# Two PSUM banks for the last block's third token group, and a front laid out in another order

## The chip, the cores and the metric

The kernel runs on one core of a Trainium2 chip. The metric is device time in microseconds (us) of one execution. The kernel before takes 789.9 us (median of three runs, 789.57 to 794.27).

## What is computed

Three stages run one behind the other, all in float32. Four batches of 576 positions with 8 heads of 64 go through an attention that works with 32 landmarks, whose small matrix is inverted by six Newton steps. Its 2304 rows of 512 then pass two feed-forward layers of width 2048:

```
q_lm, k_lm = means of 18 positions each          # 32 landmarks
A, Bm, C = sm(q, k_lm), sm(q_lm, k_lm), sm(q_lm, k)
Z = Bm.T / (norm1(Bm) * norminf(Bm))
for _ in range(6): Z = 2 * Z - Z @ Bm @ Z
x = A @ Z @ C @ v                                # as 2304 x 512
h = x @ w_in;   x = (h * clip(h + 3, 0, 6) / 6) @ w_out          # layer 1
h = x @ w2_in                                                    # layer 2
P = a0 + a1*h + a2*h**2 + a3*h**3
Q = 1 + |b0|*|h| + |b1|*h**2
out = (P / (Q + 1e-6)) @ w2_out
```

## The kernel before

Matrix products of the two layers are made of three passes each: an operand is split into a rounded high part and the rest (`hi`, `lo`), and hi x hi, hi x lo and lo x hi are added in PSUM. So each product of a 128x128 weight tile is three matmuls.

**Front.** Everything up to the seventh unit of layer 2 is written as Python generators ("steps"), each cut into pieces by `yield`. The list `ORDER` names, entry by entry, which step advances next; each engine executes its instructions in the order in which they were so written. `SLOTS` says which PSUM bank and which SBUF slab each tile of the front takes. Parts of the front that matter below: `warm` (L361, matmuls on an identity that fill waits), the attention's scores (L352), its transposes (L566, L569), `first_v` (L599, the product with v, two calls for batch 0), the Newton steps (L551 on TensorE, L588, L633 and L637 on VectorE, L631 on ScalarE), layer 1's first product (L717, with L721, L724, L727, L730 behind it) and second product (L747), its results with the first half added (L774), and the conversion of weights from raw bits (L230 on ScalarE, L236 on VectorE) and their split (L246, L249). All DMAs are issued on SP, in the same list's order.

**Layer 2.** Tokens are worked in 6 blocks (`j`) of 384, each in 8 units (`u`) of two 128-wide chunks (`i`) of the hidden dimension. For unit n, `l2_in` makes h (24 matmuls 128x384, L822), `l2_poly`, `l2_exp`, `l2_mul` and `l2_split` make the gate and its two parts, and `l2_out(n - 2)` multiplies with `w2_out`: for each of the two chunks and each of three groups of 128 tokens (`m` = 0, 1, 2), three matmuls into the group's PSUM bank `po0`, `po1`, `po2`. The sums run over all 16 chunks of a block. `po0` has two buffers, used by turns from block to block; `po1` and `po2` have one. Behind a block's last unit the banks are read out times -1 (L904 on VectorE, L906 on ScalarE) and stored (L907 on SP).

In the last block the third group is read out in two column halves, both by VectorE. Only its very last chunk (n = 47, i = 1) is also multiplied in two halves of 256 columns, into the two halves of one bank; the chunks before it are multiplied 512 columns wide.

Of the kernel before, what the change touches and what calls it, by code (L numbers as in the profile page):

```python
# [9 lines left out]
F32 = mybir.dt.float32  # L10
# [7 lines left out]
AF = mybir.ActivationFunctionType  # L18
# [9 lines left out]
DM, DFF = 512, 2048  # L28
NT = B * S
P = 128  # L30
HB = S // 2
NFC = DFF // P
NDC = DM // P
T2 = 384
NB2 = NT // T2
# [13 lines left out]


ORDER = [int(x) for x in """
# [72 lines left out]
""".split()]  # L124

SLOTS = [[int(x) for x in s.split()] for s in ("""
# [13 lines left out]
""")]  # L140

# [6 lines left out]
def fused(ctx: ExitStack, tc: tile.TileContext, qT, kT, v, w_in, w_out, w2_in, w2_out, ca, cb, out):  # L148
    nc = tc.nc
    V, A, G, PE, SP = nc.vector, nc.scalar, nc.gpsimd, nc.tensor, nc.sync  # L150
# [641 lines left out]
    L2P = {}  # L792
# [8 lines left out]
    NN = NB2 * NU2  # L801
# [73 lines left out]
    ops = {}  # L875

    def l2_out(n):
        j, u = divmod(n, NU2)
        if u == 0:
            ops[j] = [L2P["ps"].tile([P, 512], F32, tag=f"po{m}", name="po", bufs=2 if m == 0 else 1) for m in range(3)]  # L880
        t = s2.pop((n, "hl"))
        halves = [slice(0, DM // 2), slice(DM // 2, DM)]
        for i in range(2):
            c = 2 * u + i
            for m in range(3):
                for s in halves if n == NN - 1 and i == 1 and m == 2 else [slice(0, DM)]:
                    for k, (xp, wp) in enumerate(((0, 0), (0, 1), (1, 0))):
                        PE.matmul(  # L888
                            ops[j][m][:, s], t[:, xp, i, m * P:(m + 1) * P],
                            w2o[u][wp][:, i * DM + s.start:i * DM + s.stop],  # L890
                            start=(c == 0 and k == 0), stop=(c == NFC - 1 and k == 2 and s.stop == DM),
                        )
        if u == NU2 - 1:
            ps3 = ops.pop(j)

            for m in (1, 2, 0) if j < NB2 - 1 else (0, 1, 2):
                ps = ps3[m]
                o = L2P["p"].tile([P, DM], F32, tag="o", name="o", bufs=3)
                rows = out[j * T2 + m * P:j * T2 + (m + 1) * P, :]

                cs = halves if j == NB2 - 1 and m == 2 else [slice(0, DM)]
                for h, c in enumerate(cs):
                    if m == 0 or len(cs) == 2:
                        V.tensor_scalar(o[:, c], ps[:, c], -1.0, None, op0=ALU.mult)  # L904
                    else:
                        A.activation(o[:, c], ps[:, c], AF.Copy, scale=-1.0)  # L906
                    SP.dma_start(rows[:, c], o[:, c])  # L907

    def open_units():
# [35 lines left out]
    for x, j in convs:  # L945
        f, w = srcs[x]
# [85 lines left out]
    for n in range(LAID):  # L1032
        for i in cuts(n):
            at(l2_in, n, i)
            at(l2_poly, n, i, V if n == 0 or (n, i.start) == (1, 0) else G)
        for i in cuts(n - 1) if n else ():
            at(l2_split, n - 1, i)
        for i in cuts(n):
            at(l2_exp, n, i)
        for i in cuts(n):  # L1040
            at(l2_mul, n, i)
        if n >= 3:
            at(next_split, 1, n - 3)
        if n >= 2:
            at(l2_out, n - 2)
# [16 lines left out]
    for n in range(LAID, NN + 2):  # L1062
        j, u = divmod(n, NU2)
        if n < NN and u == 0 and j + 1 < NB2:
            L2P["load"](j + 1)
        for i in cuts(n):
            run(l2_in, n, i)
            run(l2_poly, n, i, G)
        for i in cuts(n - 1):
            run(l2_split, n - 1, i)  # L1070
        for i in cuts(n):
            run(l2_exp, n, i)
        for i in cuts(n):
            run(l2_mul, n, i)
        u0 = 3 if j == 0 else 2
        if n < NN and j + 1 < NB2 and u0 <= u < u0 + NDC:
            run(next_split, j + 1, u - u0)
        run(l2_out, n - 2)
# [51 lines left out]
```

## Time and profile before

| | |
|---|---|
| median of three runs | 789.9 us |
| profiled execution, its own time | 789.22 us |
| its span, first to last instruction | 787.4 us |
| TensorE busy in it | 777.1 us (99%) |
| VectorE, ScalarE, GpSimd busy | 561.7, 473.9, 323.2 us |
| granted TensorE clock | 1.0 of full speed throughout |

Matmuls overlap in the trace (a 128x512 one lasts 0.39 us and the next starts 0.23 us behind its start), so that times between starts are used below, not durations. A row that ends in "x2" merges neighbours. SPq rows are DMA issues. The engine names are PE (TensorE), DVE (VectorE), ACT (ScalarE), POOL (GpSimd) and SP.

### The profile page before, as it was taken

Reading aid. Unit: us, or ns where it says so; the run is one execution under the profiler, and the core shown is the slowest. Engines: PE = TensorE matmul, PEld = TensorE weight load, DVE = VectorE, ACT = ScalarE, POOL = GpSimd, SP = SyncE. Lnnn points to the kernel's source line nnn. Section 1 sums busy time; section 2 is a strip of 40 time slices with the busy share of each in tenths; the row PEclk is TensorE's granted clock in tenths of the full one; section 3 lists DMA queues with packets and bytes.
Section 4 is the critical chain, followed back from the end, with each engine's and each line's share of the span. In section 5 each row is a group of like instructions: output and inputs, shape, how many; then the busy total and the mean of one; then the engine's idle time right before and its main releaser. Section 6 shows DMA issues by size and latency. Waiting matters only on the chain.

```text
span 787.4 us, 15172 instructions
## 1 busy us (share of the span) xinstructions
PE 777.1 (99%) x6037; PEld 704.6 (89%) x6037; DVE 561.7 (71%) x975; ACT 473.9 (60%) x892; POOL 323.2 (41%) x230
## 2 busy tenths in 40 slices
PE   8999999999999999999999999999999999999998
PEld 3599989999899999999998889989989989989896
DVE  7888988894655477567889776765766766766665
ACT  3888746554555446567674665566656656656553
POOL 2583400000000000000289768657666765775574
PEclk9999999999999999999999999999999999999999
DMA  9998587647234666556400110110101011000001
GB/s 342 389 357 336 175 331 256 240 146 255 63 95 158 228 209 212 173 179 188 145 2 1 40 41 1 41 41 1 41 1 40 2 41 41 1 0 15 28 1 40
DMA packets 42471, 96.38 MB, mean 122 GB/s; under 512 B 5792, under 2 KB 22432, under 8 KB 42400
## 3 DMA queue, kind: packets, MB, share of 16 engines
q1 hardware_dynamic: 42400, 95.41, 35.2%
q8 instruction: 47, 0.77, 0.4%
q14 instruction: 24, 0.20, 0.1%
HBM read 73.38 MB, written 22.02 MB: 121 GB/s over the span
## 4 chain that ended last, share of the span: by engine, by line
PE 90%; DVE 6%; ACT 1%; DMA 1%; issue 1%; SPq 0%; POOL 0%; DVEq 0%; ACTq 0%
PE psy L747 25%; PE po L888 24%; PE ph L822 24%; PE psh L717 12%; PE psa L352 3%; DVE w2s L285 1%; PE psa L599 1%; DMA qx<-in_q 1%; PE psa L551 1%; DVE val L236 1%; DVE g L864 1%; DVE p L860 0%; DVE q L858 0%; PE psa L566 0%; PE psy L361 0%
## 5 line engine op out<-in xcount | busy, mean ns | idle before, releaser
L873 POOL TENSOR_TENSOR g2hl<-g,g2hl 128x768 fp32r<-128x768 f32 (+1 forms) x53 | 92.2, 1741 | 306.3 <-ACT g2hl L871 306.2
L747 PE MATMUL psy<-ghl,whi 128*128 128x288 f32 x1024 | 209.8, 298 | 0.1
L822 PE MATMUL ph<-yhl,w2h 128*128 128x384 f32 x768 | 195.7, 335 | 0.0
L888 PE MATMUL po<-w2h,g2hl 128*128 128x512 f32 x578 | 188.3, 394 | 1.3 <-POOL g2hl L873 1.2
L747 PEld LDWEIGHTS psy<-ghl,whi 128*128 128x128 f32 x1024 | 162.9, 188 | 7.8 <-issue 5.0
L747 PE MATMUL psy<-ghl,wlo 128*128 128x288 f32 x512 | 150.2, 293 | 0.0
L822 PEld LDWEIGHTS ph<-yhl,w2h 128*128 128x128 f32 x768 | 139.8, 188 | 3.8
L888 PEld LDWEIGHTS po<-w2h,g2hl 128*128 128x128 f32 x578 | 108.5, 188 | 25.4 <-POOL g2hl L873 1.9
L822 PE MATMUL ph<-yhl,w2s 128*128 128x384 f32 x384 | 128.9, 336 | 0.0
L858 DVE SCALAR_TENSOR_TENSOR q<-q,r 128x768 f32<-128x768 f32 (+1 forms) x53 | 51.6, 973 | 107.8 <-ACT r L853 106.8
L717 PE MATMUL psh<-AT,us 128*128 128x288 f32 x768 | 117.7, 296 | 0.0
L888 PE MATMUL po<-w2s,g2hl 128*128 128x512 f32 x289 | 113.4, 392 | 0.0
L717 PEld LDWEIGHTS psh<-AT,us 128*128 128x128 f32 x768 | 107.0, 188 | 0.7 <-DVE g L724 0.4
L836 POOL TENSOR_SCALAR q<-t,cab 128x768 f32<-128x768 f32 (+1 forms) x50 | 65.4, 1308 | 97.9 <-ACT t L832 97.9
L747 PEld LDWEIGHTS psy<-ghl,wlo 128*128 128x128 f32 x512 | 96.2, 188 | 0.0
L838 POOL TENSOR_TENSOR q<-q,t 128x768 f32<-128x768 f32 (+1 forms) x50 | 91.1, 1822 | 4.0
L851 ACT ACTIVATE r<-q,lnb 128x768 f32<-128x768 f32 (+1 forms) x53 | 46.5, 877 | 73.3 <-POOL q L838 72.7
L721 ACT ACTIVATE r<-psh,three 128x288 f32<-128x288 f32 x128 | 61.9, 494 | 43.7 <-PE psh L717 43.0
L727 ACT ACTIVATE ghl<-g 128x288 fp32r<-128x288 f32 x128 | 55.0, 441 | 52.6 <-DVE g L724 41.5
L832 ACT ACTIVATE t<-ph 128x384 f32<-128x384 f32 x96 | 46.9, 489 | 56.3 <-PE ph L822 56.3
L724 DVE SCALAR_TENSOR_TENSOR g<-r,psh 128x288 f32<-128x288 f32 x128 | 56.8, 449 | 31.2 <-ACT r L721 29.8
L822 PEld LDWEIGHTS ph<-yhl,w2s 128*128 128x128 f32 x384 | 72.1, 188 | 0.0
(150 smaller groups left out, 1039.9 us busy)
## 6 DMA issues: line engine op xcount, KB each, us to landing
raw<-in_moe_w_out SPq DMA_DIRECT2D x32, 511.8 KB, 6.9
raw<-in_moe_w_in SPq DMA_DIRECT2D x32, 511.5 KB, 8.0
wis<-wid SPq DMA_DIRECT2D x24, 512.0 KB, 5.1
kx<-in_k SPq DMA_DIRECT2D x8, 576.0 KB, 6.1
yd<-y SPq DMA_DIRECT2D x32, 144.0 KB, 3.4
out<-o SPq DMA_DIRECT2D x17, 256.0 KB, 2.0
vx<-in_v SPq DMA_DIRECT2D x4, 1024.0 KB, 7.9
wid<-val SPq DMA_DIRECT2D x8, 512.0 KB, 5.7
```

The costliest lines, as they stand in the source:

```text
L717: PE.matmul(ps[:, :HB], u[:, wp, f0:f0 + P], at[:, xp, g, :], start=(k == 0), stop=(k == 5))
L721: A.activation(r, ps[:, :HB], AF.Relu, bias=three)
L724: V.scalar_tensor_tensor(gg, in0=r, scalar=6.0, in1=ps[:, :HB], op0=ALU.min, op1=ALU.mult)
L727: A.activation(t[:, 0, :], gg, AF.Copy)
L747: PE.matmul(ps[e][:, :HB], w1[c // 2][wp][:, o + e * P:o + (e + 1) * P], t[:, xp, :], start=(c == c0 and i == 0), stop=(c == c1 and i == 2),)
L822: PE.matmul(ps[i][:, :T2], w2i[u][wp][:, d * 256 + i * P:d * 256 + (i + 1) * P], yh[:, xp, d, :], start=(k == 0), stop=(k == 11),)
L832: A.activation(t[:, i], h, AF.Abs)
L836: eng.tensor_scalar(q[:, cs], t[:, cs], cb_s[:, 1:2], cb_s[:, 0:1], op0=ALU.mult, op1=ALU.add)
L838: eng.tensor_tensor(q[:, cs], q[:, cs], t[:, cs], op=ALU.mult)
L858: V.scalar_tensor_tensor(q, in0=q, scalar=QC, in1=r, op0=ALU.add, op1=ALU.mult)
L873: G.tensor_tensor(t[:, 1, i], g, t[:, 0, i].bitcast(F32), op=ALU.subtract)
L888: PE.matmul(ops[j][m][:, s], t[:, xp, i, m * P:(m + 1) * P], w2o[u][wp][:, i * DM + s.start:i * DM + s.stop], start=(c == 0 and k == 0), s ...
```

## The change

First, in block 5 a fourth bank is taken, from the two buffers of `po0`; it holds columns 256 to 511 of the third group, while `po2` holds columns 0 to 255. All 16 chunks of that group are multiplied in two halves. The first half is read out by VectorE, the second by ScalarE.

```
-            ops[j] = [L2P["ps"].tile(..., bufs=2 if m == 0 else 1) for m in range(3)]
+            ops[j] = [L2P["ps"].tile(..., bufs=2 if m == 0 else 1)
+                      for m in ((0, 1, 2) if j < NB2 - 1 else (0, 1, 2, 0))]
...
-                for s in halves if n == NN - 1 and i == 1 and m == 2 else [slice(0, DM)]:
+                for h, s in enumerate(halves if j == NB2 - 1 and m == 2 else [slice(0, DM)]):
                     for k, (xp, wp) in enumerate(((0, 0), (0, 1), (1, 0))):
                         PE.matmul(
-                            ops[j][m][:, s], t[:, xp, i, m * P:(m + 1) * P],
+                            ops[j][m + h][:, s], t[:, xp, i, m * P:(m + 1) * P],
...
-                            start=(c == 0 and k == 0), stop=(c == NFC - 1 and k == 2 and s.stop == DM),
+                            start=(c == 0 and k == 0), stop=(c == NFC - 1 and k == 2),
...
-                    if m == 0 or len(cs) == 2:
+                    if m == 0 or len(cs) == 2 and h == 0:
                         V.tensor_scalar(o[:, c], ps[:, c], -1.0, None, op0=ALU.mult)
                     else:
-                        A.activation(o[:, c], ps[:, c], AF.Copy, scale=-1.0)
+                        A.activation(o[:, c], ps3[m + h][:, c], AF.Copy, scale=-1.0)
```

Second, the first part of `ORDER`, and `SLOTS` with it, holds other numbers; the rest of the table stays as it was. Two of its lines:

```
-3 5 3 6 0 3 3 8 7 3 9 123 8 12 15 124 124 125 11 16 10 10 11 11 11 10 108 2 24 25 1 11 11 11 11 108 110 25 108 11 11
+3 5 3 6 0 3 3 8 7 3 9 123 8 12 15 124 124 11 125 16 10 10 11 11 11 10 108 2 24 25 1 11 11 11 11 108 110 25 108 11 11
```

Lines behind the change move down by one: L888, L904, L906 and L907 become L889, L905, L907 and L908.

On TensorE the first difference stands in batch 0's Newton steps. Before, both calls of `first_v` (L599, writing `psa` from `vx` and `eT`) stand together, ahead of a Newton step (L551, writing `psy`) and its two fill matmuls (L361); the piece of the difference:

```order
-L599 MATMUL psa<-vx,eT 32x64 x40
-L551 MATMUL psy_431<-ev_87 32x64 x8
-L361 LDWEIGHTS ident
-L361 MATMUL psy_143<-ident 128x512
-L361 LDWEIGHTS ident
-L361 MATMUL psy_143<-ident 128x512
+L599 MATMUL psa<-vx,eT 32x64 x20
+L551 MATMUL psy_410<-ev_87 32x64 x8
+L361 LDWEIGHTS ident
+L361 MATMUL psy_143<-ident 128x512
+L361 LDWEIGHTS ident
+L361 MATMUL psy_143<-ident 128x512
+L599 MATMUL psa<-vx,eT 32x64 x20
```

The second call has moved behind that step and its fill.

On VectorE the rows between batch 1's first Newton matrix (L588, writing `ev_86`) and its second (L637) read, before:

```order
L588 SCALAR_TENSOR_TENSOR ev_86<-psa,rc,id_75 128x32 x2
L724 SCALAR_TENSOR_TENSOR g<-r,psh 128x288
L633 TENSOR_TENSOR ev_87<-ev_86,id_75 128x2x32
L542 TENSOR_SCALAR rc<-csm 128x2
L543 RECIPROCAL rc<-rc 128x2
L544 SCALAR_TENSOR_TENSOR rc<-rc 128x2
L730 TENSOR_TENSOR ghl<-g,ghl 128x288
L577 COPY eT<-psa 64x128
L730 TENSOR_TENSOR ghl<-g,ghl 128x288
L724 SCALAR_TENSOR_TENSOR g<-r,psh 128x288
L637 TENSOR_TENSOR ev_86<-psa,ev_87 128x2x64
```

and now:

```order
L588 SCALAR_TENSOR_TENSOR ev_86<-psa,rc,id_75 128x32 x2
L236 SCALAR_TENSOR_TENSOR val<-raw,top_83 128x512
L724 SCALAR_TENSOR_TENSOR g<-r,psh 128x288
L542 TENSOR_SCALAR rc<-csm 128x2
L543 RECIPROCAL rc<-rc 128x2
L544 SCALAR_TENSOR_TENSOR rc<-rc 128x2
L730 TENSOR_TENSOR ghl<-g,ghl 128x288
L774 SCALAR_TENSOR_TENSOR y<-psy,ypart 128x288
L724 SCALAR_TENSOR_TENSOR g<-r,psh 128x288
L633 TENSOR_TENSOR ev_87<-ev_86,id_75 128x2x32
L637 TENSOR_TENSOR ev_86<-psa,ev_87 128x2x64
```

L633, for which a TensorE Newton step waits, has moved from the second place behind L588 to the ninth. On TensorE, twelve matmuls L747, then eight transposes L566, now stand between the step that reads `ev_86` and the one that reads `ev_87`:

```order
L551 MATMUL psa<-ev_86 32x32 x8
L747 MATMUL psy<-ghl,whi 128x288 x2
L747 MATMUL psy<-ghl,wlo 128x288
L747 MATMUL psy<-ghl,whi 128x288 x2
L747 MATMUL psy<-ghl,wlo 128x288
L747 MATMUL psy<-ghl,whi 128x288 x2
L747 MATMUL psy<-ghl,wlo 128x288
L747 MATMUL psy<-ghl,whi 128x288 x2
L747 MATMUL psy<-ghl,wlo 128x288
L566 MATMUL psa<-ident,e 128x128 x8
L551 MATMUL psa<-ev_87 32x64 x8
```

Before, nine matmuls L747, six L717, four transposes and one L569 stood there. Likewise twelve L747 stand now between the step that makes the first matrix (L551, reading `bm`; L588 reads its result) and the step that reads `ev_86`; before it was six.

## Rows read from the trace of the kernel before

**Rows 1.** Page, part 1: busy time, share of the span and instructions by engine.

```profile
PE 777.1 (99%) x6037; PEld 704.6 (89%) x6037; DVE 561.7 (71%) x975; ACT 473.9 (60%) x892; POOL 323.2 (41%) x230
```

**Rows 2.** Waits of PE, whole span, the longest: total us, times, longest us.

```profile
PE po L888 <- POOL g2hl L873: 1.2, 1, 1.2
```

**Rows 3.** Busy time, us and (instructions), of the reordered part but its first 8 us.

```profile
core 0: us, PE busy (x) PEld busy (x) DVE busy (x) ACT busy (x) POOL busy (x), PEclk, DMA share, GB/s
30.00:115.00 85.00, 84.89 (x991) 76.55 (x986) 73.77 (x146) 64.26 (x138) 38.54 (x34) 1.00 0.84 309
```

**Rows 4.** Timeline of PE, batch 0's first product with v: start us, us, instruction.

```profile
23.64 1.13 PE L599 MATMUL psa<-vx,eT 64*32 64x64 f32 x44 [1.21 <-issue]
```

**Rows 5.** Timeline of PE, batch 1's first Newton steps (the first L551 reads bm).

```profile
95.44 0.33 PE L551 MATMUL psa<-bm 32*32 32x32 f32 x16
95.70 0.53 PE L747 MATMUL psy<-ghl,whi 128*128 128x288 f32 x2
96.07 0.29 PE L747 MATMUL psy<-ghl,wlo 128*128 128x288 f32 x1
96.20 0.42 PE L747 MATMUL psy<-ghl,whi 128*128 128x288 f32 x2
96.46 0.29 PE L747 MATMUL psy<-ghl,wlo 128*128 128x288 f32 x1
96.69 0.33 PE L551 MATMUL psa<-ev 32*32 32x32 f32 x16
96.94 0.66 PE L566 MATMUL psa<-ident,e 128*128 128x128 f32 x4
97.36 0.52 PE L747 MATMUL psy<-ghl,whi 128*128 128x288 f32 x2
```

**Rows 6.** Timeline of DVE, the same place.

```profile
96.01 0.40 DVE L588 SCALAR_TENSOR_TENSOR ev<-psa,rc,id 128x32 f32<-128x32 f32 x2
96.34 0.44 DVE L724 SCALAR_TENSOR_TENSOR g<-r,psh 128x288 f32<-128x288 f32 x1
96.70 0.21 DVE L633 TENSOR_TENSOR ev<-ev,id 128x64 f32<-128x64 f32 x1
96.83 0.16 DVE L542 TENSOR_SCALAR rc<-csm 128x2 f32<-128x2 f32 x1
...
97.30 0.45 DVE L730 TENSOR_TENSOR ghl<-g,ghl 128x288 fp32r<-128x288 f32 x1
```

**Rows 7.** Groups by form, DVE, 30 to 115: count | busy us, mean ns | idle before.

```profile
L236 DVE SCALAR_TENSOR_TENSOR val<-raw,top 128x512 uint32<-128x512 uint32 x28 | 22.1, 804 | 2.7 <-ACT top L230 2.7
```

**Rows 8.** Timeline, first second-layer output of block 5 (PE), block 4's po0 (DVE).

```profile
729.26 0.68 DVE L904 TENSOR_SCALAR o<-po 128x512 f32<-128x512 f32 x1
730.13 0.64 PE L888 MATMUL po<-w2h,g2hl 128*128 128x512 f32 x2
```

**Rows 9.** Timeline of PE, the last 57 matmuls, all on line L888: first and last.

```profile
770.81 0.39 PE L888 MATMUL po<-w2h,g2hl 128*128 128x512 f32 x1
...
782.43 0.51 PE L888 MATMUL po<-w2h,g2hl 128*128 128x512 f32 x2
782.78 0.28 PE L888 MATMUL po<-w2s,g2hl 128*128 128x256 f32 x1
...
783.25 0.28 PE L888 MATMUL po<-w2h,g2hl 128*128 128x256 f32 x1
```

**Rows 10.** Timeline, reads of the last block's second bank and third.

```profile
782.86 0.60 ACT L906 ACTIVATE o<-po 128x512 f32<-128x512 f32 x1 [3.06 <-PE po L888]
...
783.57 0.76 DVE L904 TENSOR_SCALAR o<-po 128x256 f32<-128x256 f32 x2 [0.71 <-PE po L888]
```

**Rows 11.** Timeline of SP, the last three issues: start us, us.

```profile
783.48 0.33 SPq L907 DMA_DIRECT2D out<-o  x1
...
784.02 0.33 SPq L907 DMA_DIRECT2D out<-o  x1
...
784.44 0.40 SPq L907 DMA_DIRECT2D out<-o  x1
```

More of the change, by code (lines that the diff above doesn't have):

```diff
@@ L879, in l2_out @@
         if u == 0:
-            ops[j] = [L2P["ps"].tile([P, 512], F32, tag=f"po{m}", name="po", bufs=2 if m == 0 else 1) for m in range(3)]
+            ops[j] = [L2P["ps"].tile([P, 512], F32, tag=f"po{m}", name="po", bufs=2 if m == 0 else 1)
+                      for m in ((0, 1, 2) if j < NB2 - 1 else (0, 1, 2, 0))]
         t = s2.pop((n, "hl"))
```

56 rows, old and new, of tables (ORDER, SLOTS) are left out of this document.

## The prediction

> **What bounds the kernel now.** I read the page's first part before anything else. TensorE is busy for 777.1 us of a span of 787.4 us, 99% [rows 1]; the next engine, VectorE, for 71%. So only what makes TensorE work longer or shorter, or wait, can move the time, and the two ends of the span where it doesn't work yet or any more. Next the list of TensorE's waits: the longest wait on a semaphore is 1.2 us, for GpSimd at L888 in layer 2 [rows 2], at a place that the change leaves alone. Then the window over the reordered part: from 30 to 115 us TensorE is busy 84.89 of 85.00 us, VectorE 73.77, ScalarE 64.26, and the granted clock is 1.00, full speed, 2.4 GHz [rows 3]. The reader is to see there that a better order has 0.11 us to win in these 85 us, and that VectorE, with 87% of them taken, has little room if work is put ahead of something that TensorE waits for. Last I read single rows: the start of the Newton steps, where TensorE stands idle for 1.21 us with no semaphore behind it ("issue") [rows 4], and the end, where the last matmul starts at 783.25 and lasts 0.28, to 783.53 [rows 9], so that 3.87 us of reads and stores follow it up to 787.4.
>
> The profiled execution took 789.22 us, 1.8 us more than its span; the median of the three runs is 789.9, 0.7 us above it. I work out a difference against the span and put it on the median.
>
> **The change part by part.**
>
> *Split matmuls.* Block 5 has 16 chunks; the last was split already, so 15 chunks change three matmuls of 512 columns into six of 256: 45 more instructions in pairs, the columns stay the same. Start to start, 50 intervals of 512 wide lie between 770.81 and 782.43, 0.2324 us each; from the second 256-wide start, 782.78, to the last one, 783.25, are four, 0.1175 us each [rows 9]. A pair takes 0.2350, so a split costs 0.0026 us, and 45 cost 0.12 us. This is measured on the same operands and place, so I take it. Bounds: nothing below; above, by the nearest other row, a 288-wide matmul takes half of 96.46 - 96.20, 0.13 us [rows 5], and if 256 columns took as much a split would cost 0.028 us and all of them 1.2 us.
>
> The Trainium skill speaks against splitting here: its page "TensorEngine Tiling (Array Packing)", section "Instruction Overhead", gives each matmul an overhead of about 60 cycles. If every one of the 45 added matmuls paid it, an estimate from that page's figure at 2.4 GHz is 25 ns each and 1.1 us in all, where the rows on the six halves at the end give 0.12; the trace doesn't show that overhead in matmuls that follow one another.
>
> *The fourth bank.* It is the `po0` buffer that block 4 used. VectorE reads it out from 729.26 to 729.94 [rows 8]. The second matmul of the row at 730.13 opens the third group of block 5, some 0.23 us behind, at 730.36; its first half comes first, three matmuls of 0.1175, so the new bank is written from about 730.7, 0.8 us after it is free. Cost nothing; without that lead it would be the excess of VectorE's read. Later blocks don't exist, so nothing waits for the extra bank.
>
> *The end.* Before, both halves were read after the very last matmul, since they lay in one bank with one stop: VectorE 783.57 to 784.33, two reads [rows 10]. SP issued the second group's store at 783.48, half 0's at 784.02 and half 1's at 784.44 [rows 11]; the span ends 2.96 us after this last issue. Now half 0 is complete after the third of the six 256-wide matmuls, which ends at 783.53 less three intervals, about 783.18, and VectorE reads it while TensorE still works; it is done by about 783.6. Half 1 is read by ScalarE, free since 782.86 + 0.60 = 783.46, from 783.57; it takes at most the 0.60 us of the 512-wide read [rows 10], to 784.17, and at least the 0.4 that VectorE takes for a half, to 783.97. SP limits what this gives: two issues in a row are 0.42 us apart (784.02, 784.44). So half 0's is issued at 783.90 and half 1's at 784.32, 0.12 us earlier than now. I take -0.12 us. Bounds: if SP's spacing didn't hold, 783.97 + 0.05 against 784.44 would be -0.4; if ScalarE took more than 0.72 us, nothing.
>
> *The front's order.* TensorE executes the same matmuls in it, so its length there changes only by waits and by what neighbours cost each other. The second I can price: where a run of wide matmuls is left for small ones, the start after the last wide one comes 0.23 us behind (96.46 to 96.69) instead of 0.13, and on the way back three matmuls span 0.37 (95.70 to 96.07) instead of 0.26 [rows 5]. One excursion costs 0.2 us. I counted in the two orders how often a product of layer 1 is left for small matmuls and returned to: 36 before, 35 now. That gives -0.2 us; with a doubt of two excursions either way, -0.6 to +0.2.
>
> The split of `first_v` at the start moves a Newton step between its two calls. The 1.21 us of idle stand inside the first call (44 of the row's matmuls follow it) with nothing released at its end [rows 4], so the same matmuls meet the same gap. Cost nothing; if the gap were gone, -1.2.
>
> The risky place is batch 1's first Newton matrix. VectorE's L633, which the second step reads, has moved from behind one L724 to behind seven instructions more. By durations, from L588's start: 0.40 for both L588, 0.80 for L236 [rows 7], 0.44 for L724, 0.47 for the three small ones (96.83 to 97.30), 0.45 for L730, 0.44 for L774 (priced as L724, the same 128x288 read of PSUM), 0.44 for the second L724, 0.21 for L633 [rows 6]: 3.65 us. L588 starts 0.57 us behind the step that feeds it (95.44 to 96.01), so the matrix is there 4.2 us after that step's start. TensorE, from the same start: 0.26 for the step, twelve L747 at 0.13, 0.25 for the step that reads `ev_86`, twelve more L747, and eight transposes at 0.105 (four from 96.94 to 97.36) [rows 5]: 0.26 + 1.56 + 0.25 + 1.56 + 0.84 = 4.5 us. The matrix comes 0.3 us early, so the added wait is nothing. But this holds only if VectorE reaches L588 as promptly as before. Each us by which it is later than 0.3 us is a us of TensorE; behind L633 on VectorE stand L637 of the next step and the copies of the transposes, so the next Newton steps would be late too. I take 0; bounds -0.1 (the 0.11 us of the window) and +2.5 (two of L236 and two of L724 late at once).
>
> **Sum.** +0.12 - 0.12 - 0.2 + 0 = -0.2 us. The span becomes 787.2, the profiled execution about 789.0, the median 789.7.
>
> **The rivals.**
>
> *The new order makes TensorE wait (slower than before).* At the place just described, or at a later Newton step: before, VectorE is 87% busy there [rows 3], and the lead of 0.3 us is less than one L236. For it: seven more instructions ahead of L633. Against it: the order before kept TensorE fed all through with the same load on VectorE. A lag of VectorE of 1 to 3 us there costs 0.7 to 2.7 us; in the middle 1.7, so 791.4 us. It decides from a lag of 0.3 us on. For a loss over 1% it would need 8 us of lag, ten L236 in a row.
>
> *The split costs what narrow matmuls cost elsewhere.* By the bound above 1.2 us for 0.12, so 790.8. For it: matmuls of 288 columns take 0.13. Against it: the halves of the last chunk, the very same instructions, take 0.1175. The overhead in the Trainium skill ("TensorEngine Tiling (Array Packing)", "Instruction Overhead") would make this rival true, at an estimated 790.7.
>
> *The idle at the start goes away.* With a Newton step and its fill in between, what TensorE lacked for 1.21 us would arrive behind other work [rows 4]: 789.7 - 1.2 = 788.5. For it: no semaphore ended that idle, so it can depend on what is fetched or issued just then, and the order after it is another. Against it: nothing ahead of the gap has changed on TensorE.
>
> *The end gives nothing.* If the two stores wait for each other, or ScalarE's read takes over 0.72 us, the 0.12 us are missing: 789.8, which can't be told from the forecast and is counted with it.
>
> **How the numbers follow.** The forecast, all terms as summed: 0.61; own range 789.2 to 790.3, from the bounds of the excursions and the end. A wait in the front: 0.20, 790.4 to 792.4. Costly splits: 0.06, 790.8. The idle gone: 0.13, 788.5. The range 788.2 to 792.0 takes in all but the far end of the waits. About what a measurement of this kernel can tell from no change is 1%, 7.9 us: nothing that I priced gets there. Faster by over 1% would need all of what TensorE doesn't work in the span: 0.02. Slower by over 1% needs a lag of 8 us or several waits on end: 0.04. Within 1%: 0.94.
>
> **What would show it.** Split: the intervals of 256-wide matmuls in block 5, over 45 pairs, stay at 0.1175; at 0.13 the second rival holds. Fourth bank: no wait of TensorE at its first half but one shorter than 0.1 us. End: VectorE's read of half 0 starts before the last matmul has ended, ScalarE's read follows that end by 0.04 us, and SP's last three issues stand 0.42 apart; the last comes 0.79 us after the last matmul's end instead of 0.91. Front: the 1.21 us of idle stand in the same call of `first_v`, and the first matmul of layer 2 starts 0 to 0.6 us earlier than before. A wait of TensorE at L551 on VectorE's `ev`, above all the second step of batch 1, would be the first rival. The prediction is wrong if TensorE's busy time in the reordered part falls short of its span by more than about half a us.

## The result, and the profile after

The changed kernel takes 796.0 us (median of nine runs, 793.96 to 800.85) against 789.6 us before (nine runs): a ratio of 1.0083, 95% interval 1.0055 to 1.0111. Run again beside other kernels it took 794.6 us, a ratio of 1.0057 (1.0044 to 1.0070). It is slower by 0.6 to 0.8%, and the forecast was 789.7 with a range of 788.2 to 792.0. The profiled execution took 794.1 us with a span of 792.0 us, 4.5 us more than before.

The page's first part of the kernel after, to be read beside [rows 1]:

```profile
PE 778.7 (98%) x6082; PEld 707.2 (89%) x6082; DVE 563.6 (71%) x974; ACT 473.5 (60%) x893; POOL 324.2 (41%) x230
```

TensorE is busy 1.6 us longer, so most of the 4.5 us is time in which it does nothing. The window over the reordered part, columns as in [rows 3], shows where:

```profile
30.00:115.00 85.00, 82.41 (x949) 74.19 (x942) 72.47 (x141) 61.35 (x134) 39.51 (x34) 1.00 0.84 297
```

Before, TensorE was busy 84.89 of these 85.00 us; now 2.6 us are missing. VectorE and ScalarE are less busy than before, GpSimd 1.0 us more. The list of TensorE's waits in the whole span (total us, times, longest us) names five that before did not have:

```profile
PE psy L747 <- DVE ypart L762: 0.9, 1, 0.9
PE psy L747 <- DVE ghl L730: 0.8, 2, 0.5
PE psh L717 <- DVE g L724: 0.7, 1, 0.7
PE psa L551 <- issue: 0.7, 1, 0.7
PE psy L747 <- POOL ghl L730: 0.5, 1, 0.5
```

Four of them are waits on semaphores in layer 1's products, three on VectorE and one on GpSimd. "psa L551 <- issue" has no releaser.

To put the whole difference on stages I took from each trace the time of five marks: the first L717, the first L822 (layer 2 begins), the first L822 of block 5, the end of the last matmul, and the end of the span. Stage lengths less those of before, in us (the last column is the whole span):

| kernel (median us) | to first L717 | to layer 2 | to block 5 | block 5 | behind the last matmul | span |
|---|---|---|---|---|---|---|
| before (789.6) | 31.96 | 347.93 | 328.17 | 75.47 | 3.90 | 787.4 |
| after (796.0) | -1.62 | +5.26 | +0.01 | +0.29 | +0.58 | 792.0 |
| after, again (794.6) | -0.85 | +5.26 | +0.03 | +0.29 | +0.42 | 792.6 |
| banks alone (789.9) | +1.19 | +0.37 | +0.03 | +0.29 | -0.09 | 789.2 |
| order alone (794.3) | -1.46 | +5.21 | +0.03 | 0.00 | +0.52 | 791.7 |

So the front loses 5.2 us of TensorE's time in each of three executions, and the stages that the banks change cost little. In the reordered part the long gaps between matmuls of after, each less the usual interval, are 0.91 us at 44.7, 0.75 at 72.8, 0.61 at 83.9, 1.07 at 85.3 and 0.50 at 121.3; with the gap of 0.93 at 191.8, which has no releaser, they make 4.8 of the 5.26. The other 0.5 us lie in small intervals that I did not follow. Only three of the gaps, at 44.7, 83.9 and 85.3, stand behind VectorE beside GpSimd's work, 2.6 us together; those at 72.8 and 121.3, 1.25 us, stand behind late transfers, as the experiments show.

### The profile page after: what moved, and what is told of

The parts are those of the page before. It is cut to its first block, busy times and chain, and to the rows that moved or that the text cites. A ratio compares the mean times of both kernels' runs of the same rounds, so it can differ in the third digit from the quotient of the medians.

```text
span 792.0 us, 15280 instructions
## 1 busy us (share of the span) xinstructions
PE 778.7 (98%) x6082; PEld 707.2 (89%) x6082; DVE 563.6 (71%) x974; ACT 473.5 (60%) x893; POOL 324.2 (41%) x230
## 4 chain that ended last, share of the span: by engine, by line
PE 86%; DVE 6%; DMA 5%; issue 1%; ACT 1%; SPq 0%; POOL 0%; DVEq 0%; ACTq 0%
PE po L889 24%; PE ph L822 24%; PE psy L747 23%; PE psh L717 11%; DMA raw<-in_moe_w_in 2%; PE psa L352 2%; DMA qx<-in_q 1%; DMA raw<-in_moe_w_out 1%; DVE w2s L285 1%; DVE val L236 1%; PE psa L551 1%; PE psa L599 1%; DVE g L864 1%; DVE p L860 0%; DVE q L858 0%
## 5 line engine op out<-in xcount | busy, mean ns | idle before, releaser
L747 PE MATMUL psy<-ghl,whi 128*128 128x288 f32 x1024 | 210.6, 298 | 2.2 <-DVE ypart L762 0.9
L822 PE MATMUL ph<-yhl,w2h 128*128 128x384 f32 x768 | 195.7, 335 | 0.0
L889 PE MATMUL po<-w2h,g2hl 128*128 128x512 f32 (+1 forms) x608 | 189.7, 383 | 1.4 <-POOL g2hl L873 1.2
L747 PEld LDWEIGHTS psy<-ghl,whi 128*128 128x128 f32 x1024 | 163.0, 188 | 10.3 <-issue 5.5
L747 PE MATMUL psy<-ghl,wlo 128*128 128x288 f32 x512 | 150.1, 293 | 0.0
L822 PEld LDWEIGHTS ph<-yhl,w2h 128*128 128x128 f32 x768 | 139.4, 188 | 3.3
L889 PEld LDWEIGHTS po<-w2h,g2hl 128*128 128x128 f32 x608 | 112.5, 188 | 24.4 <-POOL g2hl L873 1.9
L822 PE MATMUL ph<-yhl,w2s 128*128 128x384 f32 x384 | 128.9, 336 | 0.0
L717 PE MATMUL psh<-AT,us 128*128 128x288 f32 x768 | 118.7, 296 | 0.7 <-DVE g L724 0.7
L889 PE MATMUL po<-w2s,g2hl 128*128 128x512 f32 (+1 forms) x304 | 116.0, 382 | 0.0
L717 PEld LDWEIGHTS psh<-AT,us 128*128 128x128 f32 x768 | 107.3, 188 | 1.7 <-DVE g L724 1.0
L747 PEld LDWEIGHTS psy<-ghl,wlo 128*128 128x128 f32 x512 | 96.2, 188 | 0.0
L721 ACT ACTIVATE r<-psh,three 128x288 f32<-128x288 f32 x128 | 61.9, 494 | 43.9 <-PE psh L717 42.0
L727 ACT ACTIVATE ghl<-g 128x288 fp32r<-128x288 f32 x128 | 54.9, 440 | 48.1 <-DVE g L724 37.5
L724 DVE SCALAR_TENSOR_TENSOR g<-r,psh 128x288 f32<-128x288 f32 x128 | 56.7, 449 | 34.8 <-ACT r L721 32.3
L822 PEld LDWEIGHTS ph<-yhl,w2s 128*128 128x128 f32 x384 | 72.1, 188 | 0.0
```

The costliest lines, as they stand in the source:

```text
L717: PE.matmul(ps[:, :HB], u[:, wp, f0:f0 + P], at[:, xp, g, :], start=(k == 0), stop=(k == 5))
L721: A.activation(r, ps[:, :HB], AF.Relu, bias=three)
L724: V.scalar_tensor_tensor(gg, in0=r, scalar=6.0, in1=ps[:, :HB], op0=ALU.min, op1=ALU.mult)
L727: A.activation(t[:, 0, :], gg, AF.Copy)
L747: PE.matmul(ps[e][:, :HB], w1[c // 2][wp][:, o + e * P:o + (e + 1) * P], t[:, xp, :], start=(c == c0 and i == 0), stop=(c == c1 and i == 2),)
L822: PE.matmul(ps[i][:, :T2], w2i[u][wp][:, d * 256 + i * P:d * 256 + (i + 1) * P], yh[:, xp, d, :], start=(k == 0), stop=(k == 11),)
```

## The experiments

The theory after the traces: the new order put instructions of VectorE that read two SBUF tiles beside GpSimd's split L249, and they took longer there; such an instruction is called held below. The rows are these. First VectorE, GpSimd and TensorE of after near 84 us:

```profile
81.28 1.86 DVE L391 TENSOR_TENSOR sT<-sT,mx 128x576 f32<-128x576 f32 x1
83.06 1.54 DVE L730 TENSOR_TENSOR ghl<-g,ghl 128x288 fp32r<-128x288 f32 x1
84.70 0.45 DVE L724 SCALAR_TENSOR_TENSOR g<-r,psh 128x288 f32<-128x288 f32 x1
85.08 0.99 DVE L730 TENSOR_TENSOR ghl<-g,ghl 128x288 fp32r<-128x288 f32 x1
85.99 0.45 DVE L762 TENSOR_SCALAR ypart<-psy 128x288 f32<-128x288 f32 x1
...
80.81 6.39 POOL L249 TENSOR_TENSOR wlo<-val,whi 128x512 fp32r<-128x512 f32 x4 [0.31 <-ACT whi L246]
...
84.66 0.40 PE L747 MATMUL psy<-ghl,whi 128*128 128x288 f32 x1 [0.45 <-DVE ghl L730]
...
86.49 0.53 PE L747 MATMUL psy<-ghl,whi 128*128 128x288 f32 x2 [0.91 <-DVE ypart L762]
```

And the same two operations of VectorE before, where GpSimd's last split had ended at 87.4 us:

```profile
78.97 8.45 POOL L249 TENSOR_TENSOR wlo<-val,whi 128x512 fp32r<-128x512 f32 x6
...
89.84 0.75 DVE L391 TENSOR_TENSOR sT<-sT,mx 128x576 f32<-128x576 f32 x1
90.51 0.46 DVE L730 TENSOR_TENSOR ghl<-g,ghl 128x288 fp32r<-128x288 f32 x1
```

L391 takes 0.75 us behind GpSimd's splits and 1.86 beside them, L730 0.46 and 1.54. L724 and L762, which read at most one SBUF tile and PSUM, take 0.45 in both. The order had moved L391 from behind the run of splits into it, ahead of two L730 and an L762 for which TensorE waits. At 44.7 us the held ones are two L236, 1.78 and 1.41 us where they take 0.68 without GpSimd's reads, ahead of the L724 for which L717 waits. Being held is not new: before has an L730 of 1.22 us and an L236 of 1.79, and its mean L730 between 30 and 115 us is 560 ns, after's 576. What is new is that TensorE waits behind them.

**One part of the change at a time.** The first kernel has before's order and after's last block, the second the reverse.

> Order table of before, the two banks and the halves of after. Theory (the new order is the loss): the start keeps its 1.2 us of idle at L599, no wait of TensorE on VectorE over 1.2 us appears, the 256-wide halves start 0.118 to 0.120 us apart and the first half behind a 512-wide matmul 0.240 us behind it, so block 5 is 0.3 us longer; the end lies between 3.8 and 4.5 us behind the last matmul. Time 789.3 to 790.5, ratio within 0.15% of 1. Rival (the two banks are the loss, by the end or by the halves): 793 us or more.

Measured: 789.9 us, a ratio of 1.0004 (0.9995 to 1.0012).

> Order table of after, the last block as before. Theory (the new order is the loss): waits of TensorE between 30 and 125 us as in after (L717 on g, L747 on ghl twice or more, L747 on ypart), 3 to 5 us in all, the 1.2 us of idle at L599 absent; 793 to 796 us. The end comes 3.9 us behind the last matmul. Rival (the banks are the loss): 788 to 789.5 us.

Measured: 794.3 us, 1.0058 (1.0045 to 1.0071). The order alone is the loss; the banks can't be told from no change.

**Take away GpSimd's reads.** In both kernels:

```
-            G.tensor_tensor(lo[:, c], src[:, c], hi[:, c].bitcast(F32), op=ALU.subtract)
+            G.memset(lo[:, c].bitcast(F32), 0.0)
```

> After, with GpSimd writing zeros into the low parts of layer 1's weights in place of the subtraction L249, so that it reads nothing there (the low part of w_in and w_out of layer 1 is left out of the products; the matmuls are the same). Theory (VectorE's instructions with two SBUF inputs stand still while GpSimd's split reads SBUF, and TensorE waits for them): L236's longest falls from 1.8 to 0.7 us, L730's from 1.54 to 0.46, L391's from 1.86 to 0.75; the waits of L717 on g, of L747 on ghl by VectorE near 84 us and on ypart are gone; the wait of L747 on GpSimd's ghl near 73 us, which comes from a late transfer, and the one near 121 us behind L346 stay. 2.5 to 3.5 us less than after: 792.5 to 793.5 us by the median. Rival (VectorE is late by the place of its instructions alone): the durations fall too, but the waits stay, 795 us or more.

> Before, with the same replacement of L249 (same part left out). Theory: VectorE's long instructions become short here too, but TensorE waited for none of them: within 0.5 us of before, 789.2 to 790. Rival (GpSimd's reads hold TensorE up in any order): 788 us or less.

Measured: after without the reads 791.5 us, 1.0025 (1.0001 to 1.0050). That is 4.5 us less than after's first median, more than expected, and 3.1 us less than its second, 794.6, as expected. Before without them 790.0, 1.0007 (0.9998 to 1.0016), as expected. L730 took 450 ns on average between 30 and 115 us in the former (576 in after), L391 750 (1304). The waits at 44.7, 83.9 and 85.3 us were gone, and, against the expectation, the one near 121 us too. That one was not GpSimd's: in after it has no instruction between 112 and 126 us. There VectorE stood at L346 for a transfer of q:

```profile
118.13 1.35 DVE L346 TENSOR_REDUCE qs<-qx 128x64 f32<-128x1152 f32 x1 [1.26 <-DMA qx<-in_q]
```

Without the reads that transfer was in time. In the eight profiles of kernels with the new order, L346 stood for it 1.3 to 2.5 us in six, and in five of these TensorE then waited near 121 us (in the sixth another L346 is moved, see the rest of the order below); in the other two, this one and after's repeat, L346 didn't stand and TensorE didn't wait. So that part of what this profile gains is not the reads'. The wait at 73 us stayed and was longer. Here are ScalarE and TensorE, and two windows, of after without the reads:

```profile
72.82 0.77 ACT L230 ACTIVATE top<-raw 128x512 f16<-128x512 bf16 x1 [4.10 <-DMA raw<-in_moe_w_out]
73.46 0.47 ACT L721 ACTIVATE r<-psh,three 128x288 f32<-128x288 f32 x1
...
74.32 0.40 PE L747 MATMUL psy<-ghl,whi 128*128 128x288 f32 x1 [1.18 <-ACT ghl L727]
75.19 0.40 PE L747 MATMUL psy<-ghl,whi 128*128 128x288 f32 x1 [0.47 <-POOL ghl L730]
...
70.00:75.00 5.00, 3.54 (x48) 2.40 (x46) 1.05 (x3) 2.18 (x5) 0.66 (x1) 1.00 0.71 282
75.00:80.00 5.00, 4.81 (x24) 4.81 (x25) 5.00 (x9) 5.00 (x11) 3.07 (x7) 0.66 0.74 190
```

ScalarE stands 4.1 us at an L230 whose transfer hasn't landed, with L721 and then L727 queued behind it; VectorE and GpSimd can only follow. And behind TensorE's idle time the granted clock is 0.66 in 75 to 80 us: part of these 5 us ran at 1.2 GHz instead of 2.4, so here the wait cost a second time.

**Take away that wait.** The two entries of that conversion (step 55) are moved behind the steps of L721 and L727:

```
-... 320 46 154 55 141 318 318 55 307 312 169 43 312 ...
+... 320 46 154 141 318 318 307 312 169 55 55 43 312 ...
```

> After, with one pair of entries of the order table moved: the first half of w_out's seventh pair of rows is converted (L230 on ScalarE, L236 on VectorE) behind L721 and L727 of the next two units, not ahead of them. Theory (ScalarE stood 2.8 to 4.1 us at that L230 for a transfer, with L721 and L727 queued behind it, and TensorE waited for GpSimd's ghl near 73 us): that wait is gone and the clock stays 1.00 behind it; the waits near 45, 84 and 86 us, which come from GpSimd's reads, stay. 794 to 795 us, 1 to 2 less than after. Rival (the transfer is missed in any order, and the wait moves on): 796 us.

> After, with both: the moved conversion, and GpSimd writing zeros in place of L249 (the low part of layer 1's weights is left out). Theory (the two causes together are the whole loss of the order): no wait of TensorE over 0.5 us between 30 and 120 us, the clock 0.999 or 1.0 in nearly all runs, the spread of the times within 2 us; 788.5 to 790.5 us, as before. Rival (a third cause in the order): 791.5 us or more.

Measured: alone 795.2 us, 1.0070 (1.0057 to 1.0083); the stage to layer 2 was 5.92 us longer than before. The wait at 73 us was gone, but one of 0.6 us appeared at 78.3 (L717 on L695), and the one on L730 near 86 us grew from 0.45 to 1.22. That was the rival: the lost time moved on to the next place where VectorE was late. With both edits 790.8 us, 1.0017 (1.0000 to 1.0034), as before or little above, 0.3 us over the expected range and with a spread of 5.5 us for the expected 2; TensorE's only new wait was 0.4 us near 119 us, behind q's transfer again, and the stage to layer 2 was 1.12 us longer. So GpSimd's reads are the larger cause, 3.1 to 4.5 us by the medians. Late transfers are the other: moving the conversion won nothing clear by itself, and beside the other edit 0.7 us, which the intervals don't separate from nothing.

**Add the cause to the kernel before.** If GpSimd's reads are what holds VectorE, they must make before slow too, where VectorE has such instructions; and GpSimd's mere work must not. GpSimd is free from 88 us on there; entry 530 of the table is its last split. `scr` is a scratch tile that nothing else reads. The second kernel has twenty `G.memset(scr, 0.0)` in place of the eight.

```
+    scr = const.tile([P, 384], BF16, name="scr")
+    G.memset(scr, 0.0)
...
-    for i in ORDER:
+    for k, i in enumerate(ORDER):
         advance(steps[i])
+        if k == 530:
+            for _ in range(8):
+                G.tensor_tensor(scr, scr, scr, op=ALU.subtract)
```

> Before, with eight instructions added on GpSimd behind its last split at about 88 us, each subtracting a scratch tile (128x384, two bytes an element) from itself, read by nobody; GpSimd has no other work there. Theory (GpSimd's reads hold VectorE's instructions with two SBUF inputs): VectorE's L391 near 90 us takes 1.2 us or more instead of 0.75 and its L730 between 88 and 97 us 0.8 to 1.4 instead of 0.45, while L724 and L396, which read one SBUF input, stay at 0.44 and 0.75; TensorE waits 1 to 4 us there; 790.5 to 793.5 us. Rival (no such hold): within 0.5 us of before.

> Before, with twenty instructions added on GpSimd at the place of the eight that read, each writing zeros to the scratch tile and reading nothing. Theory (it is the reading that holds VectorE, not that GpSimd is busy): L391 near 90 us and L730 take 0.75 and 0.45 us as in before, no wait of TensorE over 0.2 us there; within 0.5 us of before. Rival (any work on GpSimd holds VectorE): as with the reads, about 3 us more than before.

Measured: with reads 793.7 us, 1.0054 (1.0041 to 1.0067), 0.2 us over the expected range; with writes, over nearly the same time, 790.1, 1.0006 (0.9991 to 1.0021). The added lines move L391 to L393, L730 to L732 and L747 to L749. With reads (VectorE, GpSimd, TensorE):

```profile
91.48 1.01 DVE L393 TENSOR_TENSOR sT<-sT,mx 128x576 f32<-128x576 f32 x1
92.42 1.07 DVE L732 TENSOR_TENSOR ghl<-g,ghl 128x288 fp32r<-128x288 f32 x1
...
87.61 8.78 POOL L1065 TENSOR_TENSOR scr<-scr 128x384 bf16<-128x384 bf16 x8
...
93.55 0.40 PE L749 MATMUL psy<-ghl,whi 128*128 128x288 f32 x1 [1.00 <-DVE ghl L732]
```

With writes (VectorE, GpSimd):

```profile
89.53 0.75 DVE L393 TENSOR_TENSOR sT<-sT,mx 128x576 f32<-128x576 f32 x1
90.20 0.45 DVE L732 TENSOR_TENSOR ghl<-g,ghl 128x288 fp32r<-128x288 f32 x1
...
87.05 9.46 POOL L1065 MEMSET scr<- 128x384 bf16 x20
```

The same instructions of VectorE take 1.01 and 1.07 us beside reads, 0.75 and 0.45 beside writes; L391 stayed under the expected 1.2. L724 and L396, with one SBUF input, stay at 0.44 and 0.74 beside reads, as expected. The stage to layer 2 is 3.23 us longer than before with reads. With writes it is 1.12 us longer in the profiled execution, without a wait on VectorE; a gap of 0.5 us without a releaser at 103 us is part of it. The Trainium skill states this in "SBUF — State Buffer", section "Who interferes with whom": a VectorE instruction with two SBUF inputs contends with a GpSimd instruction that reads SBUF, not with one that only writes it. These two runs agree, with 3.6 us between them. In every run here the GpSimd instruction that reads has two inputs; one that reads a single tile was not tried.

**Mend it in place.** In after, whole, the one entry of L391 moved behind the second L762 (step 169):

```
-50 338 313 169 322 328 313 324 322 56 316 56 324 328 47 59 58 317 58 326 ...
+50 338 313 322 328 313 324 322 56 316 56 324 328 47 59 58 317 169 58 326 ...
```

> After, whole, with one entry of the order table moved: VectorE's L391 (two SBUF inputs, 1.86 us in after beside GpSimd's split) comes behind the second L762 of that place, no longer ahead of the two L730 and that L762, for which TensorE waits. Theory: TensorE's waits on VectorE between 83 and 88 us (0.45 on ghl and 0.91 on ypart in after) fall to 0.4 us together or less; those near 45, 73 and 121 us stay; 1.0 to 1.5 us less than after. Rival (VectorE is held there by GpSimd whatever stands where): the two waits stay over 1 us together.

Measured: 793.7 us, 1.0046 (1.0033 to 1.0059), 0.9 less than after beside it (794.6); the two intervals overlap, so the gain isn't shown by the times alone. The stage to layer 2 is 1.39 us shorter than in after's two profiles. VectorE, then TensorE:

```profile
84.53 0.45 DVE L762 TENSOR_SCALAR ypart<-psy 128x288 f32<-128x288 f32 x1
84.89 1.48 DVE L391 TENSOR_TENSOR sT<-sT,mx 128x576 f32<-128x576 f32 x1
...
90.82 1.06 PE L717 MATMUL psh<-AT,us 128*128 128x288 f32 x6 [0.63 <-DVE g L724]
92.45 0.40 PE L747 MATMUL psy<-ghl,whi 128*128 128x288 f32 x1 [0.44 <-DVE ghl L730]
```

The waits of 0.45 and 0.91 us between 83 and 88 us are gone: in this trace it matters to TensorE where the held instruction stands. But L391 still takes 1.48 us, VectorE stays late, and TensorE waits 0.63 and 0.44 us at 90.8 and 92.5 instead.

**The rest of the order.** In the kernel with both edits, L346 of batch 2's keys (step 194) moved:

```
-... 350 350 350 347 66 194 348 348 352
+... 350 350 350 347 66 348 348 194 352
```

> The kernel with the moved conversion and zeros in place of L249, and besides with VectorE's L346 of batch 2's keys (1.35 us) behind the L730 that it stood ahead of near 119 us. Theory: the last wait of the order (0.4 us on ghl, 0.56 us of lost time) goes; 0.5 us less, 790.2 us, and the rest above before is the 0.3 us of the halves. Rival (L346 isn't what L730 waits for): the wait stays.

Measured: 790.9 us, 1.0004 (0.9994 to 1.0015), against the 790.8 of the kernel without this move and the expected 790.2. The wait near 119 us was gone from the trace, as expected, and VectorE stood 1.50 us for q's transfer even so. But no time was won that the runs can show: in the profiled execution a late transfer held ScalarE at L230 until 73.5 us, and TensorE waited 1.29 us at 77.5 for L693 behind it. The transfers of the new order are late by an amount that differs from one profile to the next: at that L230 ScalarE stood 2.75 us in after and 2.17 in its repeat.

> After once more, unchanged, to see which of its times repeat. Theory: the waits near 45, 84 and 86 us come again within 0.2 us; the one near 73 us, which hangs on a transfer, comes between 0.4 and 2 us and is followed by a clock below 1.00 where it is above 1.5; the idle at the start (none in the first profile, 1.2 us in before) is 0 to 2.6 us, not fixed by the order. Median 794.5 to 797.

Measured: 794.6 us. The waits of L717 near 45 us and of L747 on ypart came again at 0.7 and 0.9 us. The one on ghl near 85 us was 1.11 instead of 0.45, and the ones near 73 and 121 us did not come at all: misses. The stage to layer 2 is 5.26 us longer all the same, with 3.2 us at the three places of held VectorE instead of 2.6. The clock fell behind the pair near 86 us this time, as the last number but two shows (granted clock):

```profile
85.00:90.00 5.00, 3.60 (x16) 3.38 (x17) 4.87 (x8) 3.23 (x7) 3.71 (x4) 0.71 0.30 100
```

**The price of a split.** Before, with column halves in all blocks and groups but for a block's first chunk:

```
-                for s in halves if n == NN - 1 and i == 1 and m == 2 else [slice(0, DM)]:
+                for s in halves if c > 0 else [slice(0, DM)]:
```

> Before, with every second-layer output product cut in column halves of one bank, in all blocks and groups but for a block's first chunk: 807 more matmuls (269 triples). Theory by block 5 of after (0.289 us for 45): 6.4 ns each, 5.2 us in all, 794.5 to 795.2 us. By the six halves of before (2.6 ns): 2.1 us, 791.7. By 28 ns, the bound of the prediction: 22 us, 812.

Measured: 794.0 us, 1.0058 (1.0045 to 1.0071), between the first two. TensorE's first L822 of block 5 and its last matmul bound a stretch without any wait; first before (its last matmul is in [rows 9]), then after, then all halves:

```profile
708.06 0.51 PE L822 MATMUL ph<-yhl,w2h 128*128 128x384 f32 x2
```

```profile
711.71 0.51 PE L822 MATMUL ph<-yhl,w2h 128*128 128x384 f32 x2
...
787.20 0.28 PE L889 MATMUL po<-w2h,g2hl 128*128 128x256 f32 x1
```

```profile
712.53 0.52 PE L822 MATMUL ph<-yhl,w2h 128*128 128x384 f32 x2
...
788.64 0.28 PE L888 MATMUL po<-w2h,g2hl 128*128 128x256 f32 x1
```

That is 75.19, 75.49 and 76.11 us. With the third digit of the trace, the 45 more matmuls of after cost 0.289 us, 6.4 ns each. All halves have 168 more in the stretch (132 of block 5 and 36 of block 4's last two units, whose products run behind the mark): 0.92 us, 5.5 ns each; and the other 639, ahead of it, cost 3.47 us, 5.4 ns each. So 5.4 to 5.5 ns in one bank, 6.4 in two, and neither the 2.6 ns of the prediction nor its bound of 28.

## Why the prediction was wrong, point by point

*What bounds the kernel.* Right: TensorE bounds it, and what VectorE's order does to TensorE decides most of the loss. The prediction named the 87% load of VectorE as the danger, and the sum then set the danger at 0. One reading is wrong: the 1.2 us of [rows 2] are not the longest wait on a semaphore. The same list has a longer one on GpSimd, at the start of the span, and two waits on VectorE ahead of 30 us, L551's 1.1 us and L663's 0.7; no term hangs on it.

```profile
PE psy L361 <- POOL lnb L176: 1.5, 1, 1.5
```

*The front's order* is the step that failed. Its term for TensorE's waits stood at 0, and the stage from the first L717 to layer 2 became 5.2 us longer, by waits at five places and not at the one that was priced. The prediction's own sign of being wrong, more than half a us missing from TensorE's busy time in the reordered part, shows with 2.6. Three faults in it. First, it looked at one place only, batch 1's Newton steps, because the order's difference was plainest there. That place was worked out rightly; TensorE, then VectorE of after:

```profile
97.39 0.33 PE L551 MATMUL psa<-bm 32*32 32x32 f32 x16
...
102.34 0.43 PE L551 MATMUL psa<-ev 32*32 32x64 f32 x16
...
101.55 0.22 DVE L633 TENSOR_TENSOR ev<-ev,id 128x64 f32<-128x64 f32 x1
```

L633 ends 4.4 us behind the first step's start (forecast 4.2) and TensorE comes at 4.95 (forecast 4.5): no wait. The waits came at 45, 73, 84, 86 and 121 us, where layer 1's own chain L721, L724, L727, L730 was late: at 45, 84 and 86 behind a held VectorE, at 73 and 121 behind a late transfer. Second, VectorE's durations were taken from means over before's rows, as if they belonged to the operation. [rows 7] gave 804 ns for L236, while the shortest was 650 and the longest 1787 between 22 and 125 us; this spread was in before's trace and said that something holds VectorE at times. A duration there belongs to the operation and to what GpSimd does beside it. Third, GpSimd was not looked at at all, nor the transfers, though the table moves both.

*The rival "the new order makes TensorE wait"* was the right one in kind, with 0.20. Its price, 0.7 to 2.7 us, came from the same single place and was half of the 5.2 us that came. It decides wherever the chain ahead of TensorE is later than its lead, and there were five such places, not one. VectorE's load did not grow with it: between 30 and 115 us it is busy 72.47 us, before 73.77.

*The excursions*, -0.2 us, can't be seen beside the 0.5 us of small intervals that stay unexplained.

*The idle at the start* was taken as fixed by the order, 0 us. It is not fixed. TensorE near 23 us, after and then banks alone, whose order is before's:

```profile
23.18 0.90 PE L599 MATMUL psa<-vx,eT 128*32 128x64 f32 x40
```

```profile
24.83 0.89 PE L599 MATMUL psa<-vx,eT 64*32 64x64 f32 x36 [2.42 <-issue]
```

With before's order the idle time is 1.21 us [rows 4], 2.42 here and 0.9 to 1.1 in four more profiles; with after's order it is nothing in two profiles and 0.5 to 1.0 in six. So the rival with 0.13 came true in the profiled execution, 1.6 us to the first L717, but not as a property of the order alone. What it depends on stays open.

*Split matmuls*: right mechanism, term mis-sized, 0.29 us instead of 0.12. Six halves at the very end were too few rows: the 80 intervals from half to half in block 5 of after average 0.1198 us, for 0.1175 there. The Trainium skill's overhead of about 60 cycles for each matmul ("TensorEngine Tiling (Array Packing)", "Instruction Overhead"), by the prediction's estimate 25 ns, is not what an added matmul costs in these runs: 5.4 to 6.4 ns.

*The fourth bank*: no wait at its first use, as forecast.

*The end.* The mechanism came as described; the rows are VectorE's and SP's of banks alone, where the last matmul ends at 785.40:

```profile
785.08 0.42 DVE L905 TENSOR_SCALAR o<-po 128x256 f32<-128x256 f32 x1 [0.37 <-PE po L889]
...
785.78 0.90 SPq L908 DMA_DIRECT2D out<-o  x2
```

VectorE reads half 0 before the end, SP issues the two halves' stores at 0.38 and 0.87 us behind it (before 0.49 and 0.91, [rows 9, 11]), and the span ends 0.09 us sooner, for 0.12 forecast. SP's two issues were 0.49 apart instead of 0.42, so still less is won. In after itself the end was 0.58 us longer than before:

```profile
787.99 0.90 SPq L908 DMA_DIRECT2D out<-o  x2
```

There the two issues come 0.51 and 1.02 us behind the last matmul, and the last transfer lands 2.3 to 2.5 us behind its issue instead of 1.9. This is not the banks: order alone has it (+0.52) with before's last block. Of the fourteen profiles five have the short end (3.81 to 3.91 us) and nine the long one (4.33 to 4.52). All eight with the new order are long. Of the six with before's order five are short, but before without GpSimd's reads is long (+0.61), so the new order goes with the long end and isn't needed for it; what decides it was not found.

## What to carry to other kernels

Where an order is laid out anew, look at which engines run beside each other, not only at what stands ahead of what: an instruction of VectorE with two SBUF inputs is as long as GpSimd's reads beside it make it, here up to 1.86 us for 0.75. When one form's shortest and longest durations in the trace lie far apart, the mean is no price; find what the long ones stand beside, and check that neighbour at every place that moves. And where TensorE is 99% busy, a lateness that one place is spared can come up at the next, so that the waits must be added up over the stretch and not looked up at one step.

## What was not expected of the hardware

- GpSimd's reads, not its mere work, lengthen VectorE's two-input instructions: 1.07 us for L730 beside reads, 0.45 beside writes.
- A wait costs a second time when the clock follows: 2.1 us of lost time near 73 us without the reads, and the granted clock was 0.66 in the next 5 us; 2.3 us near 86 us in after's repeat, and it was 0.71 from 85 to 90. It does not always follow: with the moved conversion alone 2.4 us were lost between 85 and 88.5 us, and the clock stayed at 1.00. Over the changed kernel's nine runs the mean clock lay between 0.993 and 1.000, and the run at 0.993 was the slowest, 800.85 us; the four at 0.999 and 1.000 took 793.96 to 795.29. So the clock is a likely reason why the median lies 1.9 us above the profiled execution, which kept full speed, but it is not the whole: the run at 0.998 took 798.53 us, the one at 0.996 took 796.01.
- Two programs with the same last block and order ended 3.90 and 4.52 us behind the last matmul; after, profiled twice, ended 4.48 and 4.33 behind it.
